# Ordering a kernel's first pass by a deadline plan, and moving part of a weight decode from VectorE to ScalarE

## The chip, the cores and the metric

The kernel runs on one core of a Trainium2 chip. TensorE (PE) multiplies, VectorE (DVE), ScalarE (ACT) and GpSimd (POOL) do elementwise work, and SyncE (SP) issues all DMA transfers. The metric is the time of one execution on the device in microseconds, as the median of several runs.

## The reference, cut to what matters

The core computes attention and then two MoE-like blocks, all in float32:

```
attn = softmax(scale * q k^T + alibi bias, causal window of 128) @ v     # 4 x 8 heads x 576 x 64
x  = attn reshaped to (2304 tokens, 512)
h  = x @ w_in;   g = h * cos(h);                     x2  = g @ w_out      # first MoE, d_ff 2048
h  = x2 @ w_in2; g = h if h >= 1, 0 if h <= -1, else (h+1)^2/4;  out = g @ w_out2
```

## The kernel before

**Precision.** Each matrix is split in a high and a low part (both float32r), and each product takes three matmuls: high times high, high times low, low times high. The weights come in as 8-byte floats (float64 bits) and are made into float32 by bit operations; this is called the decode here. A *half* is one tile of 128 by 512 of w_in or w_out; each MoE has 32 (index `j`; `f = j // 2` from 0 to 15, even `j` is w_in, odd `j` is w_out). Two forms of the decode exist. The form with three DVE operations scales the high words on ACT (L354, L868) and then runs shift-and-mask (L374, L870), or-in the sign (L385, L873) and or-in the low bits (L389, L876) on DVE. The form with two DVE operations adds a second ACT operation that makes the last bits from a 16-bit quarter (L358), a 16-bit mask on DVE (L372), and one combining DVE operation (L382). In the first MoE halves 0 to 3 use three and halves 4 to 31 two; all 32 halves of the second MoE use three. After the decode ACT writes the high part (a cast) and DVE the low part (`sub_lo`, L282).

**Attention** (to about 123 us) is ordered by hand; `make()` advances a generator (`halves()`) by one step at some places in it, so that nearly four halves are made there. At its end `put_x(p4, "A")` copies the last block on ACT and SP stores it.

**First pass**: the first 768 tokens (chunk 0 of the first MoE) without Strassen, for each `f`: `mm_a(0, f)` (512 tokens, 12 matmuls, into bank h0), `mm_b(0, f-1)`, `mm_a(1, f)` (256 tokens), `mm_b(1, f-1)`. Between `mm_a` and `mm_b` stands `chain`: k on ACT (L603), t on DVE (L605), sine on ACT (L607), the product on DVE (L609, the last reader of the bank), high part on ACT (L616), low part on DVE. There is one bank for `mm_a(0, f)`, so the next `mm_a(0, f+1)` waits for L609. Decode steps are put in by hand between the steps of a chain (`slot()`, `needed()`); `prep` (inputs of chunk (0,1): loads, subtractions on POOL at L756, high parts on ACT at L749, 14 low parts, here all on POOL) and `sum_steps` (sums of weight pairs 0 to 2, on POOL and ACT) are collected in `todo` and emitted whole at the end of a step `f`.

**The five other chunks** ((0,1), (0,2), (1,0), (1,1), (1,2): MoE, chunk) use one level of Strassen: seven products (L946) and the second matmul (L1007). Here `Plan` orders the work: PE's order is the program's, each other operation gets a due time from the PE operation that needs it, and a simulation with a price list (`COST`) starts on each engine the most urgent operation whose inputs are ready in the simulation. The order in which the operations start there becomes each engine's queue. Engines are free from 6.0 in its time, SP from 0. A 512 KB load occupies 1.65 of its bus and lands 4.5 later. Three `ld` buffers hold raw halves. `second_weights()` decodes the second MoE's weights from 45.0 + 33.0 per pair on.

Each engine executes its queue in order. An operation that waits for an input holds all that stand behind it.

Of the kernel before, what the change touches and what calls it, by code (L numbers as in the profile page):

```python
# [19 lines left out]
TWO_PI = 6.283185  # L20
# [11 lines left out]
ROUNDED = 4  # L32


def ops(m, j):

    return 2 if m == 0 and j >= ROUNDED else 3


N_W1 = sum(ops(0, j) + 1 for j in range(2 * NF))  # L40


def needed(j):

    return min(N_W1, sum(ops(0, i) + 1 for i in range(j)) + ops(0, j) + 2)


AHEAD = 3
EARLY = 3
# [3 lines left out]
D_TAIL = 5  # L53
# [48 lines left out]
class Plan:  # L102
# [4 lines left out]
    def op(self, eng, cost, fn, reads=(), writes=(), after=0.0, gate=(), step=0):  # L107
# [6 lines left out]
        for r in writes:  # L114
            if r.writer is not None:
                o.deps.add(r.writer)
            o.deps.update(r.readers)
            if isinstance(r, Buf) and not r.users:
                o.new.append(r)
            r.writer, r.readers = o, []  # L120
# [123 lines left out]
def attention_moe_moe_kernel(  # L244
# [48 lines left out]
    def stage_raw(m, j):  # L293

        if j < 2 * NF and (m, j) not in raw64:
# [40 lines left out]
    def halves():  # L336

        before = None  # L340

        def new_u(j):
            f = j // 2
            if j % 2:
                return two.tile([128, 512], F32, tag="wu", name=nm("wu"), bufs=U_BUFS)
            if f % 2 == 0:
                win_u[f // 2] = big("W", NF, "up", F32, (128, 4, 256)) if f < 12 else pair_tile()
            return half_u(win_u[f // 2], f)

        def first(j):  # L350
            stage_raw(0, j)
            low, high = words(raw64[0, j])
            u = new_u(j)
            ACT.activation(u, high.bitcast(F32), AF.Copy, scale=2.0**-112)  # L354
            if ops(0, j) == 2:


                ACT.activation(low.bitcast(I32), quarters(raw64[0, j])[:, :, 1], AF.Copy,  # L358
                               bias=0.5**14 - 0.5, scale=0.5**13)
            return u  # L360

        u = first(0)
        yield
        for j in range(2 * NF):
            stage_raw(0, j + 1)
            t = raw64.pop((0, j))
            low, high = words(t)
            ui = u32(u)
            if ops(0, j) == 2:

                q = quarters(t)
                DVE.tensor_single_scalar(out=q[:, :, 1], in_=q[:, :, 3], scalar=0x8000, op=ALU.bitwise_and)  # L372
            else:
                DVE.tensor_scalar(out=ui, in0=ui, scalar1=3, scalar2=0x7FFFFFFF,  # L374
                                  op0=ALU.logical_shift_left, op1=ALU.bitwise_and)
            yield
            if before:
                before()
                yield
            if ops(0, j) == 2:  # L380
                u_next = first(j + 1) if j + 1 < 2 * NF else None
                DVE.scalar_tensor_tensor(out=ui, in0=ui, scalar=3, in1=low,  # L382
                                         op0=ALU.logical_shift_left, op1=ALU.bitwise_or)
            else:
                DVE.scalar_tensor_tensor(out=ui, in0=high, scalar=0x80000000, in1=ui,  # L385
                                         op0=ALU.bitwise_and, op1=ALU.bitwise_or)
                yield
                u_next = first(j + 1) if j + 1 < 2 * NF else None
                DVE.scalar_tensor_tensor(out=ui, in0=low, scalar=29, in1=ui,  # L389
                                         op0=ALU.logical_shift_right, op1=ALU.bitwise_or)  # L390
            f, h = j // 2, j % 2
# [6 lines left out]
            def before(w=w, u=u, f=f, h=h):  # L398
                sub_lo(DVE, w[:, 1, :], u, w[:, 0, :])
                if not h:  # L400
                    p = f // 2
                    if f % 2:
                        if p >= EARLY:
                            stores.append(lambda: SP.dma_start(ud[p], win_u[p]))
                        stores.append(lambda: move(fd[0][p][3], w[:, :, 256:512]))
                    else:
                        stores.append(lambda: move(fd[0][p][0], w))

            yield
            u = u_next  # L410
        if before:
            before()
            yield

    making = halves()
    made = [0]
    started = [False]

    def start():

        if not started[0]:
            started[0] = True
            next(making)

    def make():

        start()
        if next(making, making) is not making:
            made[0] += 1


# [149 lines left out]
    c0 = {}  # L581

    def mm_a(i, f):
        tag = "h3" if f == 1 and i == 0 else f"h{i}"
        w = FIRST[i][1]
        h = ps.tile([128, 512], F32, tag=tag, name=nm("h"))[:, 0:w]
        n = 0
        for d in range(KD):
            xh, xl = x0[i, d]
            s = slice(d * 128, d * 128 + 128)  # L590
            for k, x in ((0, xh), (0, xl), (1, xh)):
                PE.matmul(h, lhsT=win[f][:, k, s], rhs=x, start=(n == 0), stop=(n == 11))  # L592
                n += 1
        c0["h", i, f] = h

    def chain(i, f):


        w, h = FIRST[i][1], c0.pop(("h", i, f))
        t = small("t")[:, 0:w]  # L600
        k = small("k", I32)[:, 0:w]

        ACT.activation(k, h, AF.Copy, bias=0.25, scale=INV_2PI)  # L603
        yield
        DVE.scalar_tensor_tensor(out=t, in0=h, scalar=INV_2PI, in1=k,  # L605
                                 op0=ALU.mult, op1=ALU.subtract)
        ACT.activation(t, t, AF.Sin, bias=half_pi, scale=TWO_PI)  # L607
        yield
        DVE.tensor_tensor(out=t, in0=h, in1=t, op=ALU.mult)  # L609
        if i:  # L610
            g = small("g", F32R)
            gh, gl = g[:, 0:w], g[:, w:2 * w]
        else:
            gh, gl = (small(s, F32R)[:, 0:w] for s in ("gh", "gl"))
        c0["g", i, f] = gh, gl
        ACT.copy(gh, t)  # L616
        yield
        sub_lo(DVE, gl, t, gh)

    def mm_b(i, f):  # L620
        if f == 0:
            w = FIRST[i][1]
            if i:
                b = [ps.tile([128, 512], F32, tag=f"h{2 + d}", name=nm("y")) for d in range(2)]
                c0["y", i] = [b[d // 2][:, d % 2 * w:d % 2 * w + w] for d in range(KD)]
            else:
                c0["y", i] = [ps.tile([128, 512], F32, tag=f"y{d}", name=nm("y"))[:, 0:w]
                              for d in range(KD)]
        gh, gl = c0["g", i, f]

        for d in range(KD):
            s = slice(d * 128, d * 128 + 128)
            for k, (a, x) in enumerate(((0, gh), (0, gl), (1, gh))):
                PE.matmul(c0["y", i][d], lhsT=wout[f][:, a, s], rhs=x,
                          start=(f == 0 and k == 0 and not (i and d % 2)),
                          stop=(f == NF - 1 and k == 2 and (i == 0 or d % 2 == 1)))

# [8 lines left out]
    def attention():  # L646
# [8 lines left out]
        for k in range(-AHEAD, np_ - AHEAD - 1):  # L655
# [35 lines left out]
            if k + 1 == D_STEPS[0]:  # L691
                start()
# [37 lines left out]
        for _ in range(D_TAIL - 2):  # L730
            make()
        put_x(p4, "A")

# [48 lines left out]
    def first_pass():  # L782

        todo = {}

        def later(eng, cost, fn, reads=(), writes=(), gate=(), step=0):
            new = [r for r in writes if isinstance(r, Buf) and not r.users]
            for r in new:
                r.users.append(None)

            def run():
                for r in new:
                    r.t = r.make()
                fn()

            todo.setdefault(step, []).append(run)

        bt = prep(later, 0, 1, "P", (), 5)
        for b in bt.values():
            for t in b:  # L800
                t.users.clear()
        for p in range(EARLY):
            s = Buf("W", None)
# [363 lines left out]
```

## Time and profile before

| | |
|---|---|
| median of 3 runs | 924.61 us (922.9 to 925.96) |
| profiled execution: its own time | 919.17 us |
| profiled execution: span | 917.4 us, granted clock 0.994 |
| PE busy | 882.2 us (96%) |
| DVE busy | 676.9 us (74%) |
| ACT busy | 534.9 us (58%) |
| POOL busy | 272.4 us (30%) |
| DMA | 190.29 MB, mean 207 GB/s |

The 2 us between the span and the execution's own time lie around the span. PE counts as busy also while it runs slower than it could, so the share of 96% says little; the stages have to be read apart. A name such as "DVE gl L282" is an engine, the tile written and the line.

### The profile page before, as it was taken

What the parts mean: (1) busy time and instruction counts of PE and PEld (TensorE: products, weight loads), DVE (VectorE), ACT (ScalarE), POOL (GpSimd) and SP (SyncE); (2) the same over time, 40 slices, a digit from 0 to 9 for tenths busy, and PEclk for the clock granted to TensorE, in tenths of its full rate; (3) what the DMA queues carried; (4) which work ended last, traced back from release to release, by engine and by line L of the source; (5) the groups of instructions that cost most, each with busy time, mean ns of one, the idle gap of its engine ahead of it and who ended that gap; (6) DMA issues with size and microseconds to landing.
All of it is one profiled execution on the core that took longest, in us unless ns stands there. A gap on an engine that the chain in (4) does not pass through costs nothing.

```text
span 917.4 us, 15799 instructions
## 1 busy us (share of the span) xinstructions
PE 882.2 (96%) x5472; PEld 829.1 (90%) x5472; DVE 676.9 (74%) x1429; ACT 534.9 (58%) x1225; POOL 272.4 (30%) x276
## 2 busy tenths in 40 slices
PE   7998999988899999899999999999999999999998
PEld 5776778877789999889999989999999999999998
DVE  7997888878867779988898998776555558355551
ACT  8886878767656666557666565555344445344440
POOL 5766730364334532671210760201200004000000
PEclk9999999999999999999999999999999999999999
DMA  9547545757569978759879769865155452444200
GB/s 321 166 146 232 186 159 176 259 204 248 171 212 322 333 284 298 240 204 347 298 249 336 243 218 341 291 203 176 52 195 161 165 160 82 138 161 161 93 35 34
DMA packets 81262, 190.29 MB, mean 207 GB/s; under 512 B 8224, under 2 KB 40992, under 8 KB 81184
## 3 DMA queue, kind: packets, MB, share of 16 engines
q1 hardware_dynamic: 81184, 189.30, 60.8%
q8 instruction: 43, 0.70, 0.3%
q14 instruction: 35, 0.29, 0.1%
HBM read 140.51 MB, written 48.76 MB: 206 GB/s over the span
## 4 chain that ended last, share of the span: by engine, by line
PE 49%; DVE 6%; issue 2%; ACT 1%; POOL 0%; DVEq 0%; ACTq 0%
PE y L1007 26%; PE h L946 24%; DVE gl L282 2%; DVE wu L873 1%; DVE wu L870 1%; DVE wo L282 1%; DVE up L870 0%; DVE b L282 0%; ACT gh L964 0%; DVE up L876 0%; POOL T L756 0%; ACT c L954 0%; DVE t L987 0%; DVE t L975 0%; DVE t L981 0%
## 5 line engine op out<-in xcount | busy, mean ns | idle before, releaser
L1007 PE MATMUL y<-gh,wo 128*128 128x384 f32 x1280 | 338.6, 335 | 0.0
L946 PE MATMUL h<-b,wi 128*128 128x384 f32 x1680 | 308.2, 336 | 6.2 <-DVE b L282 2.7
L946 PEld LDWEIGHTS h<-b,wi 128*128 128x128 f32 x1680 | 292.6, 188 | 9.8 <-ACT c L954 4.4
L1007 PEld LDWEIGHTS y<-gh,wo 128*128 128x128 f32 x1280 | 232.7, 188 | 0.1
L1007 PE MATMUL y<-gl,wo 128*128 128x384 f32 x640 | 214.8, 336 | 4.1 <-DVE gl L282 4.1
L1007 PEld LDWEIGHTS y<-gl,wo 128*128 128x128 f32 x640 | 120.4, 188 | 6.3 <-DVE gl L282 6.3
L954 ACT COPY c<-h 128x384 f32<-128x384 f32 x120 | 57.3, 477 | 92.2 <-PE h L946 88.3
L958 DVE TENSOR_TENSOR c<-h,c 128x384 f32<-128x384 f32 x120 | 66.4, 554 | 47.2 <-PE h L946 26.8
L324 POOL TENSOR_TENSOR up<-up 128x256 f32<-128x256 f32 x64 | 60.2, 943 | 129.8 <-DVE so L282 113.9
L984 ACT ACTIVATE t<-t,half 128x384 f32<-128x384 f32 x96 | 58.9, 617 | 56.5 <-DVE t L981 56.1
L282 DVE TENSOR_TENSOR gl<-t,gh 128x384 fp32r<-128x384 f32 (+1 forms) x96 | 61.2, 638 | 33.7 <-ACT gh L964 28.3
L592 PE MATMUL h<-x,wi 128*128 128x512 f32 (+1 forms) x384 | 75.1, 347 | 9.7 <-DVE t L609 9.7
L507 ACT ACTIVATE sc<-sc,st 128x256 f32<-128x256 f32 (+1 forms) x144 | 70.2, 489 | 21.1 <-DVE st L500 19.4
L513 POOL TENSOR_TENSOR sc<-sc,st 128x512 f32<-128x512 f32 (+1 forms) x72 | 70.0, 994 | 36.8 <-DVE st L644 24.4
L592 PEld LDWEIGHTS h<-x,wi 128*128 128x128 f32 x384 | 62.0, 195 | 19.3 <-DVE t L609 10.5
L756 POOL TENSOR_TENSOR xs<-xs,xs 128x384 f32<-128x384 f32 x20 | 25.4, 1270 | 172.0 <-DVE b L282 121.5
L282 POOL TENSOR_TENSOR so<-up,so 128x512 fp32r<-128x512 f32 x32 | 47.0, 1478 | 90.1 <-ACT so L328 90.1
L282 DVE TENSOR_TENSOR gl<-g,gh 128x384 fp32r<-128x384 f32 x80 | 55.0, 727 | 6.7 <-PE y L1007 3.1
L994 DVE TENSOR_TENSOR g<-c,t 128x384 f32<-128x384 f32 x80 | 48.0, 600 | 15.7 <-ACT t L984 10.1
L500 DVE CUSTOM_DVE_ANT_0 sc<-pa,dist 128x256 f32<-128x256 f32 (+1 forms) x144 | 52.5, 403 | 8.1 <-PE pa L485 7.8
L978 ACT ACTIVATE t<-t,half_pi 128x384 f32<-128x384 f32 x64 | 39.4, 616 | 27.1 <-DVE t L975 26.5
L964 ACT CAST gh<-t 128x384 fp32r<-128x384 f32 x80 | 41.1, 514 | 23.5 <-DVE t L987 22.6
(94 smaller groups left out, 1226.9 us busy)
## 6 DMA issues: line engine op xcount, KB each, us to landing
wi<-fd SPq DMA_DIRECT2D x120, 512.0 KB, 4.5
wst<-in_w SPq DMA_DIRECT2D x64, 512.0 KB, 4.7
fd<-so SPq DMA_DIRECT2D x40, 512.0 KB, 4.3
qk<-in_qkv SPq DMA_DIRECT2D x36, 320.0 KB, 3.6
wi<-fd SPq DMA_DIRECT2D x40, 256.0 KB, 3.1
xs<-xd SPq DMA_DIRECT2D x40, 192.0 KB, 4.0
v<-in_qkv SPq DMA_DIRECT2D x36, 192.0 KB, 3.8
out_t<-ys SPq DMA_DIRECT2D x24, 192.0 KB, 1.9
```

Of the source, the lines that this page charges most:

```text
L282: eng.tensor_tensor(out=out, in0=full, in1=f32(hi), op=ALU.subtract)
L324: op("P", "tt256", lambda i=i, x=x, y=y, alu=alu: POOL.tensor_tensor(out=s.t[:, i, :], in0=s.t[:, x, :], in1=s.t[:, y, :], op=alu), writes ...
L500: DVE.tensor_tensor_reduce(out=sc[:, h, 0:w], in0=b[h], in1=dist8[2 * hp + h][:, 256 - w:256], scale=-0.125, scalar=3.0e38, op0=ALU.add, o ...
L507: ACT.activation(sc[:, h, 0:w], sc[:, h, 0:w], AF.Exp, bias=st[:, c:c + 1], scale=-1.0, accum_out=st[:, 4 + c:5 + c])
L513: POOL.tensor_tensor(out=sc[:, :, 0:w], in0=sc[:, :, 0:w], in1=st[:, 8 + 2 * j:10 + 2 * j].unsqueeze(2).to_broadcast([128, 2, w]), op=ALU. ...
L592: PE.matmul(h, lhsT=win[f][:, k, s], rhs=x, start=(n == 0), stop=(n == 11))
L946: PE.matmul(cell.t, lhsT=unit.t[:, a, s], rhs=bs[kt].t[:, x, :], start=(start and i == 0), stop=(stop and i == 5), skip_group_check=True)
L954: op("A", "copy384", lambda: ACT.copy(s.t, cell.t), reads=[bank[tag]], writes=[s])
L958: op("D", "tt384", lambda: DVE.tensor_tensor(out=s.t, in0=cell.t, in1=s.t, op=ALU.add), reads=[bank[tag]], writes=[s])
L984: op("A", "f384", lambda: ACT.activation(t.t, t.t, AF.Square, bias=half, scale=0.5), writes=[t])
L994: DVE.tensor_tensor(out=g.t, in0=h.t, in1=t.t, op=alu)
L1007: PE.matmul(cell.t, lhsT=w[:, a, s], rhs=x.t, start=(first and i == 0 and k == 0), stop=(last and i == 1 and k == 2), skip_group_check=True)
```

## The change

The hand order of the first pass goes (`first_pass`, `slot`, `needed`, `later`). `rest` becomes `moes`: the first pass's matmuls, chains, decodes, `prep` and `sum_steps` are handed to the same `Plan` as the rest, ahead of the other chunks. PE's order stays as it was. In attention four halves are made to their end, their stores issued, and nothing of half 4. `prep` of chunk (0,1) splits its 14 low parts between DVE and POOL. The decode of the second MoE takes the form with two DVE operations, and starts at 178.0 + 33.0 per pair, in a plan whose time now begins at the end of attention.

```diff
+MADE = 4
+W2_FROM, W2_STEP = 178.0, 33.0
 COST: "A": + k512 (0.49, 0.66), f512 (0.57, 0.78), k256 (0.29, 0.43), f256 (0.41, 0.56)
       "D": + ts16 (0.72, 0.82)
...
 def halves():
-        for j in range(2 * NF):
-            stage_raw(0, j + 1)
+        for j in range(MADE):
+            stage_raw(0, j)
+            if j + 1 < MADE:
+                stage_raw(0, j + 1)
...
+            ACT.activation(u, high.bitcast(F32), AF.Copy, scale=2.0**-112)
             yield
+            DVE.tensor_scalar(out=ui, ..., op0=ALU.logical_shift_left, op1=ALU.bitwise_and)
+            yield
+            DVE.scalar_tensor_tensor(out=ui, in0=high, ...)
+            yield
+            DVE.scalar_tensor_tensor(out=ui, in0=low, ...)
...
+            ACT.copy(w[:, 0, :], u)
+            if before:
+                yield
+                low_part(*before)
+            before = f, h
...
 # end of attention()
         put_x(p3, "A")
         make()
-        for _ in range(D_TAIL - 2):
-            make()
+        for _ in making:
+            pass
         put_x(p4, "A")
+        while stores:
+            stores.pop(0)()
...
+    def moes():
-                    {"s": [13.0] * 7, "W": w_held, "B": [...],
-                     "Q": [6.0], "so": [8.0] * 2, "up": [9.0] * 2, "wu": [6.0] * 2})
+                    {"s": [8.0] * 4, "ld": [9.0], "wu": [8.0], **kept})
+        def decode(raw, u, ap):            # for both MoEs
+            op("A", "u512", lambda: ACT.activation(ap(), words(raw.t)[1].bitcast(F32), ...), reads=[raw], writes=[u])
+            op("A", "u512", lambda: ACT.activation(words(raw.t)[0].bitcast(I32), quarters(raw.t)[:, :, 1], ...), writes=[raw])
+            op("D", "ts16", lambda: DVE.tensor_single_scalar(out=quarters(raw.t)[:, :, 1],
+                in_=quarters(raw.t)[:, :, 3], scalar=0x8000, op=ALU.bitwise_and), writes=[raw])
+            op("D", "tt512", lambda: DVE.scalar_tensor_tensor(out=u32(ap()), in0=u32(ap()), scalar=3,
+                in1=words(raw.t)[0], ...), reads=[raw], writes=[u])
...
-                start = 45.0 + 33.0 * p
+                start = W2_FROM + W2_STEP * p
...
+        def first_weights(j):
+            raw = Buf("ld", ...)
+            op("S", "512", lambda: SP.dma_start(raw.t, w1[f, h]), writes=[raw])
+            ...
+            decode(raw, u, ap)
+            op("A", "hi512", ..., reads=[u], writes=[w])
+            op("D", "tt512", lambda: sub_lo(DVE, ...), reads=[u], writes=[w])
...
+        sum_steps(op, 0, 0, pair0, ...)
+        for f in range(NF):
+            if 2 * f >= MADE:
+                first_weights(2 * f)
+                first_weights(2 * f + 1)
+            mm_a(0, f)
+            chain(0, f)
+            if f:
+                mm_b(0, f - 1)
+            last = mm_a(1, f)
+            chain(1, f)
+            for g in (f - 2, f - 1) if f == 2 else (f - 1,) if f > 2 else ():
+                mm_b(1, g)
+            if f == 4:
+                bt = prep(op, 0, 1, "DP", [last])
         for p in range(EARLY, NP):
             s = Buf("up", pair_tile)
-            load_sum(op, p, s, ())
+            load_sum(op, p, s, [ud_res[p]])
...
         attention()
-        rest(first_pass())
+        moes()
```

## Rows read from the trace of the kernel before

**Rows 1.** Busy time by stage (us busy, x instructions, clock, DMA share, GB/s).
```profile
123.06:268.56 145.50, 134.66 (x747) 116.74 (x746) 120.13 (x183) 104.05 (x203) 49.65 (x40) 0.98 0.62 210
...
374.00:412.00 38.00, 33.07 (x183) 31.07 (x182) 35.31 (x45) 19.59 (x42) 28.07 (x23) 1.00 0.59 198
...
503.00:550.00 47.00, 44.18 (x240) 42.59 (x239) 43.95 (x56) 27.13 (x57) 32.34 (x27) 0.96 0.70 235
550.00:917.00 367.00, 363.98 (x2100) 363.66 (x2098) 212.31 (x419) 155.64 (x314) 24.96 (x22) 1.00 0.46 153
```

**Rows 2.** Timeline of PE, first pass (start us, us).
```profile
123.06 7.24 PE L592 MATMUL h<-x,wi 128*128 128x512 f32 x36
130.80 0.50 PE L634 MATMUL y<-gh,wo 128*128 128x512 f32 x1 [0.51 <-ACT gh L616]
...
146.38 2.91 PE L592 MATMUL h<-x,wi 128*128 128x512 f32 x12
...
154.72 2.91 PE L592 MATMUL h<-x,wi 128*128 128x512 f32 x12
...
192.11 4.37 PE L592 MATMUL h<-x,wi 128*128 128x512 f32 x12 [3.87 <-DVE t L609]
...
241.80 4.61 PE L592 MATMUL h<-x,wi 128*128 128x512 f32 x12 [2.68 <-DVE t L609]
...
268.56 1.21 PE L946 MATMUL h<-b,wi 128*128 128x384 f32 x6
```

**Rows 3.** Waits in 125 to 275 us (total, times, longest us).
```profile
PE h L592 <- DVE t L609: 9.7, 4, 3.9
```

**Rows 4.** Timeline of ACT in front of the longest stall.
```profile
186.89 0.51 ACT L749 CAST b<-xs 128x384 fp32r<-128x384 f32 x1 [2.98 <-POOL xs L756]
...
188.35 0.59 ACT L603 ACTIVATE k<-h 128x512 int32<-128x512 f32 x1
```

**Rows 5.** Timeline of ACT where attention ends.
```profile
122.62 0.68 ACT L354 ACTIVATE wu<-wst 128x512 f32<-128x512 f32 x1
123.20 0.61 ACT L396 CAST wi<-up 128x512 fp32r<-128x512 f32 x1
123.72 0.36 ACT L570 COPY x<-pa 128x256 f32<-128x256 f32 x1
126.21 0.60 ACT L603 ACTIVATE k<-h 128x512 int32<-128x512 f32 x1 [2.13 <-PE h L592]
126.95 0.68 ACT L354 ACTIVATE up<-wst 128x512 f32<-128x512 f32 x1
```

**Rows 6.** Timeline of SP's DMA queue, the same stretch.
```profile
123.12 0.42 SPq L297 DMA_DIRECT2D wst<-in_w  x1
124.11 0.32 SPq L574 DMA_DIRECT2D xd<-x  x1
```

**Rows 7.** DMA issues from 110 to 140 us (median us to landing).
```profile
wst<-in_w SPq DMA_DIRECT2D x5, 512.0 KB, 3.9
```

**Rows 8.** Lines of the decode: duration ns min/median/max, first and last start.
```profile
L372 DVE TENSOR_SCALAR wst<-wst x28: 729/761/1468, 128.2 to 253.9; 128x512 uint16<-128x512 uint16 x28
...
L382 DVE SCALAR_TENSOR_TENSOR wu<-wu,wst x14: 682/1506/1789, 135.2 to 255.7; 128x512 uint32<-128x512 uint32 x14
...
L870 DVE TENSOR_SCALAR up<-up x16: 415/424/1227, 324.9 to 567.5; 128x512 uint32<-128x512 uint32 x16
...
L876 DVE SCALAR_TENSOR_TENSOR up<-wst,up x16: 677/684/1501, 327.3 to 573.5; 128x512 uint32<-128x512 uint32 x16
...
L358 ACT ACTIVATE wst<-wst x28: 639/660/696, 127.5 to 253.3; 128x512 int32<-128x512 uint16 x28
```

**Rows 9.** Timeline of DVE at 190 us.
```profile
190.08 1.47 DVE L372 TENSOR_SCALAR wst<-wst 128x512 uint16<-128x512 uint16 x1 [0.42 <-ACT wst L358]
```

**Rows 10.** Timeline of POOL at 188 us.
```profile
188.45 2.51 POOL L282 TENSOR_TENSOR so<-up,so 128x512 fp32r<-128x512 f32 x2
```

**Rows 11.** Timeline of PE, end of chunk (0,1).
```profile
383.75 0.44 PE L1007 MATMUL y<-gl,wo 128*128 128x384 f32 x1 [1.62 <-DVE gl L282]
```

More of the change, by code (lines that the diff above doesn't have):

```diff
@@ L117, in op @@
             o.deps.update(r.readers)
-            if isinstance(r, Buf) and not r.users:
+            if isinstance(r, Buf) and not r.users and r.make:
                 o.new.append(r)
@@ L293, in stage_raw @@
     def stage_raw(m, j):
-        if j < 2 * NF and (m, j) not in raw64:
+        if (m, j) not in raw64:
             t = two.tile([128, 512], mybir.dt.int64, tag="ld", name=nm("wst"), bufs=LD_BUFS)
@@ L336, in halves @@
     def halves():
-        before = None
[L342 to L350, printed above, removed]
-            stage_raw(0, j)
[L352 to L360, printed above, removed]
@@ L380, in halves @@
[L380 to L390, printed above, removed]
@@ L391, in halves @@
-            f, h = j // 2, j % 2
+            if h:
+                wout_u[f] = u = two.tile([128, 512], F32, tag="wu", name=nm("wu"), bufs=U_BUFS)
+            else:
+                if f == 0:
+                    win_u[0] = big("W", NF, "up", F32, (128, 4, 256))
+                u = half_u(win_u[0], f)
+            ui = u32(u)
+            ACT.activation(u, high.bitcast(F32), AF.Copy, scale=2.0**-112)
+            yield
+            DVE.tensor_scalar(out=ui, in0=ui, scalar1=3, scalar2=0x7FFFFFFF,
+                              op0=ALU.logical_shift_left, op1=ALU.bitwise_and)
@@ L392, in halves @@
+            yield
+            DVE.scalar_tensor_tensor(out=ui, in0=high, scalar=0x80000000, in1=ui,
+                                     op0=ALU.bitwise_and, op1=ALU.bitwise_or)
+            yield
+            DVE.scalar_tensor_tensor(out=ui, in0=low, scalar=29, in1=ui,
+                                     op0=ALU.logical_shift_right, op1=ALU.bitwise_or)
             if h:
@@ L396, in halves @@
             ACT.copy(w[:, 0, :], u)
[L398 to L413, printed above, removed]
-    making = halves()
[L416 to L423, printed above, removed]
+            if before:
+                yield
+                low_part(*before)
+            before = f, h
+        yield
+        low_part(*before)
+    wout_u = {}
+    making = halves()
     def make():
-        start()
-        if next(making, making) is not making:
-            made[0] += 1
+        next(making, None)
     def kind(blk):
@@ L579, in attention_moe_moe_kernel @@
     half_pi2 = one.tile([128, 1], F32, name="half_pi2")
[L581 to L636, printed above, removed]
     def prepare(p):
@@ L780, in load_sum @@
         op("S", "512", lambda: SP.dma_start(s.t, ud[p]), reads=reads, writes=[s])
[L782 to L803, printed above, removed]
-            s.users.append(None)
-            early = lambda *a, step=0, p=p, **k: later(*a, step=step + 2 * p + 2, **k)
-            early("P", "", lambda s=s, p=p: setattr(s, "t", win_u[p]))
-            sum_steps(early, 0, p, s, lambda: Buf("so", part_tile), lambda i: Res())
-        def slot():
-            if made[0] < N_W1:
-                make()
-        for f in range(NF):
-            while made[0] < needed(2 * f):
-                make()
-            mm_a(0, f)
-            for _ in chain(0, f):
-                slot()
-            if f:
-                mm_b(0, f - 1)
-            mm_a(1, f)
-            for n, _ in enumerate(chain(1, f)):
-                if n:
-                    slot()
-            slot()
-            while made[0] < needed(2 * f + 1):
-                make()
-            for g in (f - 2, f - 1) if f == 2 else (f - 1,) if f > 2 else ():
-                mm_b(1, g)
-            for fn in todo.pop(f, ()):
-                fn()
-        for f in sorted(todo):
-            for fn in todo[f]:
-                fn()
-        while stores:
-            stores.pop(0)()
-        return bt
-    def rest(bt):
-        w_held = []
+    def moes():
         bank = {f"{k}{i}": Res() for k in "hy" for i in range(4)}
@@ L845, in rest, with ready @@
         wo = [[None] * NF for _ in range(2)]
-        for f in range(NF):
-            wo[0][f] = b = Buf("W", None)
-            b.t = wout[f]
-            w_held.append(b)
+        wi = [None] * NF
+        held = []
+        def ready(tag, t):
+            b = Buf(tag, None)
+            b.t = t
+            held.append(b)
+            return b
+        for f in range(2):
+            wo[0][f] = ready("W", wout[f])
+            wi[f] = ready("Q", win[f])
+        pair0 = ready("W", win_u[0])
         g_res = [Res() for _ in range(NF)]
@@ new lines, in moes, with mm_a, go @@
+        h_of, g_of, y_of = {}, {}, {}
+        def mm_a(i, f):
+            tag = "h3" if f == 1 and i == 0 else f"h{i}"
+            w = FIRST[i][1]
+            cell = h_of[i, f] = Cell()
+            def go():
+                cell.t = h = ps.tile([128, 512], F32, tag=tag, name=nm("h"))[:, 0:w]
+                n = 0
+                for d in range(KD):
+                    xh, xl = x0[i, d]
+                    s = slice(d * 128, d * 128 + 128)
+                    for k, x in ((0, xh), (0, xl), (1, xh)):
+                        PE.matmul(h, lhsT=wi[f].t[:, k, s], rhs=x, start=(n == 0), stop=(n == 11))
+                        n += 1
+            cell.res = bank[tag]
+            return op("PE", f"b{w}", go, reads=[wi[f]], writes=[cell.res])
@@ new lines, in chain @@
+        def chain(i, f):
+            w, h = FIRST[i][1], h_of.pop((i, f))
+            t, k = Buf("s", lambda: small("t")[:, 0:w]), Buf("s", lambda: small("k", I32)[:, 0:w])
+            op("A", f"k{w}", lambda: ACT.activation(k.t, h.t, AF.Copy, bias=0.25, scale=INV_2PI),
+               reads=[h.res], writes=[k])
+            op("D", f"tt{w}", lambda: DVE.scalar_tensor_tensor(
+                out=t.t, in0=h.t, scalar=INV_2PI, in1=k.t, op0=ALU.mult, op1=ALU.subtract),
+               reads=[h.res, k], writes=[t])
+            op("A", f"f{w}", lambda: ACT.activation(t.t, t.t, AF.Sin, bias=half_pi, scale=TWO_PI), writes=[t])
+            op("D", f"tt{w}", lambda: DVE.tensor_tensor(out=t.t, in0=h.t, in1=t.t, op=ALU.mult),
+               reads=[h.res], writes=[t])
+            if i:
+                gs = [Buf("s", lambda: small("g", F32R))]
+                part = lambda n: gs[0].t[:, n * w:n * w + w]
+            else:
+                gs = [Buf("s", lambda: small("gh", F32R)), Buf("s", lambda: small("gl", F32R))]
+                part = lambda n: gs[n].t
+            g_of[i, f] = gs, part
+            op("A", f"hi{w}", lambda: ACT.copy(part(0), t.t), reads=[t], writes=gs[:1])
+            op("D", f"tt{w}", lambda: sub_lo(DVE, part(1), t.t, part(0)), reads=[t, gs[0]], writes=gs[-1:])
@@ new lines, in mm_b, with go @@
+        def mm_b(i, f):
+            w = FIRST[i][1]
+            tags = ["h2", "h3"] if i else [f"y{d}" for d in range(KD)]
+            gs, part = g_of.pop((i, f))
+            def go():
+                if f == 0:
+                    b = [ps.tile([128, 512], F32, tag=tag, name=nm("y")) for tag in tags]
+                    y_of[i] = [b[d // 2][:, d % 2 * w:d % 2 * w + w] if i else b[d][:, 0:w] for d in range(KD)]
+                for d in range(KD):
+                    s = slice(d * 128, d * 128 + 128)
+                    for k, (a, x) in enumerate(((0, 0), (0, 1), (1, 0))):
+                        PE.matmul(y_of[i][d], lhsT=wo[0][f].t[:, a, s], rhs=part(x),
+                                  start=(f == 0 and k == 0 and not (i and d % 2)),
+                                  stop=(f == NF - 1 and k == 2 and (i == 0 or d % 2 == 1)))
+            return op("PE", f"b{w}", go, reads=[wo[0][f], *gs], writes=[bank[t] for t in tags])
```

115 lines of the change are left out of this document (65 added, 50 removed), and 4 rows, old and new, of the table COST.

## Prediction

> **What bounds the kernel now.** I read the busy time by stage first. From 550 us on PE runs 2100 matmuls of 384 columns in 363.98 us, 0.1733 us each, with no stage below that pace but the last few microseconds [rows 1]: nothing that only reorders work can gain there. The losses lie ahead of it. In 374 to 412 us, where chunk (0,1) hands over to (0,2), 183 matmuls need 31.7 of 38 us: 6.3 lost. In 503 to 550 us, the hand-over from (0,2) to (1,0), 240 need 41.6 of 47: 5.4 lost. In both DVE is busy for 93% of the time (35.31 of 38, 43.95 of 47) [rows 1], and PE's waits there are for a low part on DVE [rows 11].
>
> The first pass runs from 123.06 to 268.56 us, 145.5 us [rows 1, 2]. PE's timeline gives its undisturbed step: `mm_a(0, f)` starts at 146.38 and the next at 154.72, 8.34 us apart. There are 16 groups `mm_a` and 15 groups `mm_b`, two of which make a step: 15.5 x 8.34 = 129.3 us. So 16.2 us are lost. Four waits of `mm_a` for the product L609 make 9.7 of them [rows 3]. After the two longer ones (3.87 and 2.68 us) the 12 matmuls take 4.37 and 4.61 us where others take 2.91 [rows 2], and the granted clock of the pass is 0.98 and not 1.00 [rows 1]: 3.2 more, 12.9 in all. The other 3.3 lie at the start and in small pieces.
>
> Why L609 is late, ACT's timeline shows: ACT stood 2.98 us in front of a cast of `prep` that waited for POOL's subtraction, and the k of the chain, which needs only PE, came behind it at 188.35 [rows 4]. The longest wait, 3.87 us, follows from that. It is a fault of the order, not of the amount of work: ACT is busy for 104.05 of 145.5 us and DVE for 120.13 [rows 1].
>
> **The change, part by part.** *The order of the first pass.* `Plan` starts an operation only when its inputs are ready in its simulation, so a cast that needs POOL isn't put ahead of a k that is ready. The four waits go: 12.9 us off. Bounds: 0 if all come back in another place, 12.9; I take the full amount, since ACT has 41 us to spare in the pass and the plan knows what each cast waits for.
>
> *The start of the first pass.* Here the plan is wrong about SP. It lets SP issue the loads of halves 4 and 5 at its time 0, six units before PE, and has them land before k of `chain(0, 0)` is ready; so ACT's queue gets u of half 4, its last bits, u of half 5, and only then k. On the chip SP's queue stands behind attention's last transfers. Before, the load of half 4 was issued at 123.12, ahead of the store of `put_x(p4)` at 124.11 [rows 6]; now it comes behind that store. And `put_x(p4)` itself, an ACT copy at 123.72 [rows 5], now comes behind all of half 3: u 0.68, from about 123.2, then shift, sign and low bits on DVE (0.42, 0.68, 0.68 by their medians [rows 8]), the cast 0.61, the copy 0.36 [rows 5], and about 0.5 of hand-overs: 127.1. Then three issues of about 0.4 each [rows 6] (the x store, a store of half 2's factor, the load of half 4) bring that load to about 128, and 3.9 us to landing [rows 7] to about 132; half 5 is there by 132.6, its u done by 133.3. k of `chain(0, 0)` then starts at 133.3 instead of 126.21 [rows 5]. From k to `mm_b(0, 0)` it took 4.59 us (130.80 [rows 2]), so that group starts at 137.9. PE has work until about 130.2 and now waits 7.7 us instead of 0.5: 7.2 more, and 1.5 for the clock after such a wait (4.37 against 2.91 [rows 2]). Cost: 8.7. Bounds: 0, if the loads are there in time, and 8.7. Behind k on ACT stand the sine and the high part of the same chain, and PE waits for them. The halves 4 and on lose nothing more, since PE waits longer than they do.
>
> *`prep`'s low parts.* Seven go from POOL to DVE. No row gives one alone; the DVE operations of 512 columns bound it by 0.42 and 1.50 us [rows 8]: 3 to 10.5 us for seven, I take 6.4, near 0.9 each. DVE idles for 25.4 us of the pass [rows 1], which hides them; without that cover they cost what the third rival says. Finishing half 3 inside attention moves three DVE operations of about 0.7 us forward by 2 to 3 us, behind which the chain waited anyway.
>
> *The second MoE's decode.* Per half L870, L873 and L876 go (0.42 + 0.69 + 0.68 = 1.79 us by their medians, L873 priced like L876) and L372 and L382 come (0.76 + 0.68, the least of L382): 0.35 us less DVE. When POOL runs beside them the longest are 1.23 + 1.50 + 1.50 = 4.23 against 1.47 + 1.51 (L382's median) = 2.98: 1.25 less [rows 8]. The stretches that start a pair (four halves) every 33 us hold 4.6 and 5.7 halves: 1.6 to 5.8 us in the first, 2.0 to 7.1 in the second. Both are bound by DVE, so I take the low end as the gain, 3.6 together; the bounds are 0 and 11.7, all that is lost there. ACT pays 0.66 us (L358) for each of 32 halves, 21 us, hidden under its idle time (19.59 busy of 38, 27.13 of 47 [rows 1]). If that cover is gone, a half comes late, and it is next needed only in chunk (1,0), or when a third raw buffer has to come free.
>
> One row speaks for how much of this is saved. L372 at 190.08 took 1.47 us while POOL ran a low part from 188.45 to 190.96 [rows 9, 10], twice its median of 0.76: as if it waited for POOL, although it reads one tile. The Trainium skill ("SBUF — State Buffer", Who interferes with whom) says that a DVE instruction with at most one SBUF input outside the two-port modes does not contend with GpSimd, and that one with two SBUF inputs does. By that rule L372 would cost 0.76 beside POOL too, and the saving there would be 1.96 us a half and not 1.25. The row goes against it, so the sum stays by rows.
>
> Where the second MoE's decode starts hardly moves: 172 after PE's start in the new plan, 39 after the start of chunk (0,1) in the old one, and the first pass is 129.3 to 145.5 long.
>
> Sum: -12.9 + 8.7 - 3.6 = -7.8 us. On the profiled execution 919.17 gives 911.4; that execution is 5.4 below the median, so on the median's scale 924.61 gives 916.8.
>
> **The rivals.**
>
> *No wait at the start.* If the load of half 4 lands before k is ready, the 8.7 us don't come: 924.61 - 12.9 - 3.6 = 908.1. For it: before, that load landed by 126.95, when its u began without waiting [rows 5]. Against it: the order of SP's queue.
>
> *Other waits take the place of the old ones.* The plan's queues are fixed by its prices; where an operation takes twice its price, as beside POOL [rows 8], what stands behind it is late. If the start costs 8.7, and one wait of the old kind with its slow clock (3.87 + 1.5) is left, the time is 924.61 - 7.8 + 5.4 = 922.2, and with the gain at the hand-overs gone too 925.8; I put the case at 924, no change that can be measured.
>
> *DVE becomes the bound of the first pass: slower.* DVE has 120.13 us of work there, and 6.4 are added: 126.5 [rows 1]. At today's share of 83% that takes 153 us, 7.7 more than now, less 3.6 later: 928.7. The plan also may pull sums of pairs 3 and up into the pass, and their POOL time stretches DVE's. It decides when DVE can't be kept busy for more than 126.5 / 149.1 = 85% of the pass. Against it: in the two hand-overs DVE was kept busy for 93%.
>
> **How the numbers follow.** Forecast (start costs, waits gone, 912 to 921): 0.42. No wait at the start (904 to 911): 0.20. Other waits (921 to 927): 0.17. DVE the bound (927 to 932): 0.15. Outside these, 0.06, mostly below 904 or a worse hand-over. About 0.3%, 2.8 us, is what a measurement of this kernel can tell from no change. Faster than 921.8: nearly all of the first two and a quarter of the third, 0.68; same 0.16; slower 0.16. The range 904 to 926 leaves out DVE the bound and little else; the forecast's own is 912 to 921.
>
> **What would show it.** In the changed kernel's trace: the load of half 4 issued after the store of `put_x(p4)`; ACT's k of `chain(0, 0)` behind two u's, near 133; `mm_b(0, 0)` near 138; no wait over 1 us of `mm_a` for L609's successor after that, and from there steps of 8.34; DVE's idle time in the pass small but there; at the two hand-overs PE's loss down from 6.3 and 5.4 to about 8 together. The prediction is wrong if `mm_b(0, 0)` starts before 133, if waits for DVE are spread over the pass, or if the second half of the kernel, from 550 us on, does not keep its pace.

## The result, and the profile after

The changed kernel takes 914.04 us (median; 912.6 to 916.26) and the kernel before, in the same rounds, 924.37 (922.9 to 925.96): a ratio of 0.989, 95% interval 0.9864 to 0.9916. The forecast was 916.8. The total came out, but by luck: two of its terms were each off by about 6 us, in opposite directions.

Busy time by stage of the kernel after, its stages cut like those of [rows 1]: the first pass, then 105.45 us, the first hand-over, 91 us, the second hand-over, and the rest (columns as there).

```profile
127.47:275.05 147.58, 133.66 (x746) 115.97 (x745) 130.09 (x190) 107.95 (x211) 68.25 (x59) 0.98 0.74 253
275.05:380.50 105.45, 104.88 (x606) 104.05 (x604) 78.61 (x138) 71.92 (x146) 17.83 (x18) 1.00 0.75 254
380.50:418.50 38.00, 37.40 (x211) 36.19 (x211) 35.11 (x44) 24.34 (x52) 26.87 (x21) 1.00 0.67 236
418.50:509.50 91.00, 91.00 (x527) 91.00 (x526) 74.33 (x129) 67.44 (x137) 17.10 (x16) 1.00 0.85 296
509.50:556.50 47.00, 44.62 (x244) 43.32 (x243) 42.45 (x55) 26.77 (x56) 27.44 (x24) 0.96 0.74 251
556.50:914.40 357.90, 354.52 (x2046) 354.20 (x2044) 204.87 (x402) 155.63 (x314) 27.50 (x22) 1.00 0.45 150
```

And two stretches of the kernel before that [rows 1] leave out:

```profile
268.56:374.00 105.44, 103.70 (x591) 101.31 (x590) 83.87 (x138) 67.40 (x139) 39.49 (x36) 1.00 0.86 307
412.00:503.00 91.00, 90.23 (x520) 89.78 (x519) 78.29 (x143) 62.10 (x126) 18.04 (x17) 1.00 0.87 306
```

The first pass takes 147.58 us against 145.5 [rows 1, 2]: it became 2.1 longer, where 4.2 less were forecast. From its end to the end of the span it is 639.4 us against 917.4 - 268.56 = 648.8: 9.5 less, where 3.6 were forecast. The matmul counts say where: in stretches as long as before, PE gets through 15, 28, 7 and 4 matmuls more. At 0.1733 us each [rows 1] that is 2.6, 4.9, 1.2 and 0.7 us, 9.4 in all. The last stage keeps its pace.

PE's timeline at the start of the first pass (as [rows 2]):

```profile
127.47 7.20 PE L786 MATMUL h<-x,wi 128*128 128x512 f32 x36
142.09 0.79 PE L825 MATMUL y<-gh,wo 128*128 128x512 f32 x1 [7.43 <-ACT gh L810]
...
147.02 3.21 PE L786 MATMUL h<-x,wi 128*128 128x256 f32 x19
```

SP's DMA queue at the end of attention (as [rows 6]):

```profile
118.09 13.31 SPq L518 DMA_DIRECT2D xd<-x  x6
131.49 0.62 SPq L278 DMA_DIRECT2D fd<-wi  x1
132.16 7.10 SPq L747 DMA_DIRECT2D wst<-in_w  x4
```

ACT's timeline there (as [rows 5]):

```profile
130.69 0.36 ACT L514 COPY x<-pa 128x256 f32<-128x256 f32 x1
136.17 0.66 ACT L700 ACTIVATE up<-wst 128x512 f32<-128x512 f32 x1 [5.12 <-DMA wst<-in_w]
136.74 0.63 ACT L702 ACTIVATE wst<-wst 128x512 int32<-128x512 uint16 x1
137.28 0.58 ACT L795 ACTIVATE k<-h 128x512 int32<-128x512 f32 x1
```

Read these from bottom to top. PE's 7.43 us wait is for the chain of k, and k is ready work: its matmuls ended near 130. It stands behind two operations on half 4, these behind a load, and the load at 132.16 behind the stores of a factor and of attention's last block, whose copy ACT makes only at 130.69. No engine is short of time there (from 127.47 to 142.09 DVE is busy for 6.87 of 14.62 us and ACT for 6.51); by this reading the order of two queues makes the wait, which e1, e5, e9 and e10 test. The granted clock of 142.09 to 147.02 is 0.58, near the lower level of 1.2 GHz, after PE stood still.

The waits of PE in the pass (columns as [rows 3]) show that the wait for t, L609 then and L801 now, fell from 9.7 to 4.5 us, in five pieces of at most 1.5:

```profile
PE y L825 <- ACT gh L810: 7.4, 1, 7.4
PE h L786 <- DVE t L801: 4.5, 5, 1.5
PE y L825 <- DVE g L271: 1.9, 2, 1.0
```

### The profile page after: what moved, and what is told of

Read it like the earlier page. It is cut to its first block, busy times and chain, and to the rows that moved or that the text cites. A ratio compares the mean times of both kernels' runs of the same rounds, so it can differ in the third digit from the quotient of the medians.

```text
span 914.4 us, 15792 instructions
## 1 busy us (share of the span) xinstructions
PE 882.4 (96%) x5472; PEld 832.2 (91%) x5472; DVE 668.9 (73%) x1404; ACT 552.9 (60%) x1257; POOL 264.2 (29%) x269
## 5 line engine op out<-in xcount | busy, mean ns | idle before, releaser
L313 POOL TENSOR_TENSOR up<-up 128x256 f32<-128x256 f32 x64 | 62.2, 972 | 212.2 <-DVE so L271 170.2
L786 PE MATMUL h<-x,wi 128*128 128x512 f32 (+1 forms) x384 | 72.3, 339 | 4.5 <-DVE t L801 4.5
L786 PEld LDWEIGHTS h<-x,wi 128*128 128x128 f32 x384 | 59.9, 190 | 13.8 <-DVE t L801 5.8
L271 DVE TENSOR_TENSOR gl<-g,gh 128x384 fp32r<-128x384 f32 x80 | 59.3, 778 | 7.2 <-PE y L937 3.1
L705 DVE TENSOR_SCALAR wst<-wst 128x512 uint16<-128x512 uint16 x60 | 52.3, 871 | 10.9 <-ACT wst L702 10.4
```

What stands on the lines that cost most here:

```text
L271: eng.tensor_tensor(out=out, in0=full, in1=f32(hi), op=ALU.subtract)
L313: op("P", "tt256", lambda i=i, x=x, y=y, alu=alu: POOL.tensor_tensor(out=s.t[:, i, :], in0=s.t[:, x, :], in1=s.t[:, y, :], op=alu), writes ...
L705: op("D", "ts16", lambda: DVE.tensor_single_scalar(out=quarters(raw.t)[:, :, 1], in_=quarters(raw.t)[:, :, 3], scalar=0x8000, op=ALU.bitwi ...
L786: PE.matmul(h, lhsT=wi[f].t[:, k, s], rhs=x, start=(n == 0), stop=(n == 11))
```

## The experiments

For each run, from its profile: the length of the first pass, the time from there to the end of the span ("later part"), and the timed ratio to the kernel before. c0_after is the changed kernel run once more, as a yardstick. A ratio is taken to the kernel before in the same rounds; its median there was 924.37 us for after, 921.31 for e1 to e4, 922.20 for c0_after, e5, e7 and e8, and 920.50 for e9 to e11. So compare ratios, not medians.

| run | pass | later part | median us | ratio (95%) |
|---|---|---|---|---|
| before (span 917.4) | 145.5 | 648.8 | 924.37 | 1 |
| after (span 914.4) | 147.6 | 639.4 | 914.04 | 0.989 (0.9864 to 0.9916) |
| c0_after | 148.3 | 639.4 | 913.18 | 0.9903 (0.9889 to 0.9918) |
| e1_loads_early | 145.3 | 638.6 | 910.91 | 0.988 (0.9861 to 0.9898) |
| e2_decode3 | 148.8 | 645.2 | 919.23 | 0.9965 (0.995 to 0.9979) |
| e3_before_decode2 | 145.6 | 641.7 | 914.38 | 0.9912 (0.9894 to 0.9929) |
| e4_sums_late | 142.2 | 639.8 | 909.95 | 0.986 (0.984 to 0.9879) |
| e5_sp_time | 155.4 | 638.6 | 919.99 | 0.9981 (0.9965 to 0.9997) |
| e7_k_first | 141.5 | 645.5 | 910.27 | 0.9868 (0.9851 to 0.9885) |
| e8_prep_pool | 150.6 | 639.3 | 918.73 | 0.9956 (0.9938 to 0.9973) |
| e9_sum0_held | 135.9 | 640.0 | 902.48 | 0.98 (0.9774 to 0.9825) |
| e10_plan_times | 138.8 | 638.0 | 902.04 | 0.9804 (0.9778 to 0.983) |
| e11_dve_back | 144.9 | 651.8 | 923.82 | 1.0031 (1.0013 to 1.0049) |

My theory after the result: the decode's DVE time makes the gain, the order of the start and POOL's work inside the pass eat what the planned order brings. The rival: the planned order makes the gain and the decode little.

**The two parts, each alone: e2, e3.** e2 is the changed kernel with the old decode of the second MoE:

```diff
-                decode(raw, u, ap)
+                decode3(raw, u, ap)    # u512 on ACT; ts512, tt512, tt512 on DVE
```

> The changed kernel, with the second MoE decoded by three DVE operations again and nothing else undone. Theory A (the hand-overs gained by fewer DVE operations): PE's loss in the hand-over from chunk (0,1) to (0,2), 1.4 us now against 6.3 before the change, returns by 3 us or more, and the kernel takes about 918 to 921. Theory B (they gained by the new order and the pair sums that moved into the first pass): the loss stays under 3 us and the time is 913 to 916.

e3 is the kernel before with the new decode in `second_weights`, and the price of `ts16` in the plan (shortened):

```diff
-  ts512, tt512, tt512 on DVE
+  op("A", "u512", ...)   # last bits on ACT
+  op("D", "ts16", ...)
+  op("D", "tt512", ...)
```

> The kernel before the change, with the second MoE decoded by two DVE operations and one more ACT operation: that part of the change alone. Theory A (decode): the hand-over from chunk (0,1) to (0,2) loses 2 us or less of PE time instead of 6.3, and the kernel takes about 917 to 920. Theory B (order): 922 to 925.

The decode alone gives 0.88%, about 8 us, and everything but the decode (e2, called the order here) 0.35%; together 1.2%, about what the whole change gives. In e2 the pass is 3.3 us longer than in the kernel before, the later part 3.6 shorter. Why the order alone shortens the later part was not taken apart. The times speak for theory A, its sign at the first hand-over less so: by the matmul count at 0.1733 us PE's loss there returns from 1.4 to 4.0 us in e2 (196 matmuls), a little less than expected, and in e3 it is 5.4 (188 matmuls) and not under 2. The two hand-overs of e3 (stages as above):

```profile
374.21:412.21 38.00, 34.70 (x188) 33.78 (x188) 33.85 (x41) 22.31 (x47) 25.68 (x23) 0.96 0.61 207
503.21:550.21 47.00, 45.99 (x262) 44.89 (x261) 45.87 (x59) 30.38 (x62) 30.92 (x25) 1.00 0.74 255
```

Here the second one gains (262 matmuls for 240), in the kernel after it is the first (211 for 183). The split between the two depends on the order and stays open.

**Is it DVE's time? e11.** e3, with one DVE operation given back per half that leaves the bits as they are:

```diff
+  op("D", "ts512", lambda: DVE.tensor_scalar(out=u32(ap()), in0=u32(ap()),
+      scalar1=0, scalar2=0xFFFFFFFF, op0=ALU.logical_shift_left, op1=ALU.bitwise_and))
   op("D", "ts16", ...)
   op("D", "tt512", ...)
```

> The kernel before with the new decode of the second MoE, which alone gave a ratio of 0.991, and one DVE operation more per half (a shift by 0 and a mask of ones, 0.42 us), so that DVE's work per half is that of the kernel before. If DVE's time is what the decode saved, the gain goes: ratio 0.996 to 1.002. If it came from something else in the new form (the order that the plan makes of it, or shorter use of the raw buffers), the ratio stays at 0.990 to 0.994.

The gain is gone: 1.0031, just above the expected range, and a later part of 651.8 against 641.7 of e3. ACT's operation was still in, so the gain goes with DVE's operations and not with ACT's. The added operation also holds the raw buffer longer and changes the plan's order; the run doesn't separate these. How far DVE's time fell, the groups of DVE's instructions show (busy us, mean ns). Before, for 32 halves in 290 to 620 us:

```profile
L873 DVE SCALAR_TENSOR_TENSOR wu<-wst,wu 128x512 uint32<-128x512 uint32 x16 | 13.5, 851 | 0.2
L876 DVE SCALAR_TENSOR_TENSOR wu<-wst,wu 128x512 uint32<-128x512 uint32 x16 | 13.3, 837 | 0.1
L876 DVE SCALAR_TENSOR_TENSOR up<-wst,up 128x512 uint32<-128x512 uint32 x16 | 12.6, 785 | 0.0
...
L873 DVE SCALAR_TENSOR_TENSOR up<-wst,up 128x512 uint32<-128x512 uint32 x16 | 11.9, 741 | 0.3
L870 DVE TENSOR_SCALAR wu<-wu 128x512 uint32<-128x512 uint32 x16 | 9.7, 606 | 0.5 <-ACT wu L868 0.5
...
L870 DVE TENSOR_SCALAR up<-up 128x512 uint32<-128x512 uint32 x16 | 8.8, 548 | 1.3 <-ACT up L868 1.3
```

After, in 300 to 620 us:

```profile
L705 DVE TENSOR_SCALAR wst<-wst 128x512 uint16<-128x512 uint16 x32 | 26.4, 824 | 4.0 <-ACT wst L702 3.8
...
L708 DVE SCALAR_TENSOR_TENSOR wu<-wu,wst 128x512 uint32<-128x512 uint32 x16 | 17.8, 1139 | 0.0
...
L708 DVE SCALAR_TENSOR_TENSOR up<-up,wst 128x512 uint32<-128x512 uint32 x16 | 11.5, 720 | 0.1
```

69.8 against 55.7 us: 14.1 us, 0.44 a half. PE gained 9.4 us from these 14.1 and from the order. In e11 the decode takes DVE longer than in the kernel before:

```profile
L876 DVE TENSOR_SCALAR wst<-wst 128x512 uint16<-128x512 uint16 x32 | 27.1, 855 | 0.6 <-ACT wst L870 0.2
...
L879 DVE SCALAR_TENSOR_TENSOR wu<-wu,wst 128x512 uint32<-128x512 uint32 x16 | 15.4, 962 | 0.1
...
L879 DVE SCALAR_TENSOR_TENSOR up<-up,wst 128x512 uint32<-128x512 uint32 x16 | 14.5, 906 | 0.1
...
L873 DVE TENSOR_SCALAR wu<-wu 128x512 uint32<-128x512 uint32 x16 | 10.1, 638 | 0.5 <-ACT wu L868 0.5
...
L873 DVE TENSOR_SCALAR up<-up 128x512 uint32<-128x512 uint32 x16 | 9.2, 576 | 1.1 <-ACT up L868 0.9
```

That is 76.3 us, 6.5 more than before, and its later part is 3.0 us longer. In e3 the same groups take 54.8 us, 15.0 less, and the later part is 7.1 us shorter; in e2 they take 66.2, 10.5 more than in the kernel after, and the later part is 5.9 us longer. In all three pairs a microsecond of DVE in the decode is worth about half a microsecond of the later part (0.46, 0.47, 0.56), which is the best support here for DVE's time as the cause.

**The start: e1, e5.** e1 issues the loads of halves 4 and 5 in attention's tail, as the kernel before did with half 4:

```diff
+        for j in range(MADE, MADE + 2):
+            stage_raw(0, j)
...
+            raw = early_raw.get(j)
+            if raw is None: ...    # else no load here
```

> The changed kernel, with the raw halves 4 and 5 loaded ahead of the last copy and store of attention, and told to the plan as already there. Theory (SP's queue order makes the start wait): mm_b(0,0) starts within 4 us of the end of the third mm_a instead of 7.4 us after it, the PE wait of 7.4 us and the slow matmuls after it (about 2 us) go, and the kernel runs in about 905 to 907 us. Rival (the wait is ACT's and DVE's backlog from attention, or the decode of later halves is then late instead): a wait of more than 4 us stays or comes back within the first steps, and the time stays above 911.

ACT's timeline in e1:

```profile
128.83 0.67 ACT L703 ACTIVATE up<-wst 128x512 f32<-128x512 f32 x1 [0.39 <-DMA wst<-in_w]
130.14 0.66 ACT L703 ACTIVATE wu<-wst 128x512 f32<-128x512 f32 x1 [0.64 <-DMA wst<-in_w]
130.70 1.21 ACT L705 ACTIVATE wst<-wst 128x512 int32<-128x512 uint16 x2
131.80 0.59 ACT L800 ACTIVATE k<-h 128x512 int32<-128x512 f32 x1
```

The loads now hardly stop ACT, and k starts 6.95 us after PE's first `mm_a` (124.85 in e1) instead of 9.81; it still stands behind four operations on halves 4 and 5. PE's wait falls to 4.38 us and not to nothing, and the waits for t rise to 7.2 us in six pieces. The ratio can't be told from c0_after's, and the expected 905 to 907 us were missed. The late load makes 3 of the 7.4 us of wait; the rest is order, as e9 and e10 show, where k goes first.

e5 tells the plan that SP is free only at 11.0:

```diff
-        free["S"] = 0.0
+        free["S"] = 11.0
```

> The changed kernel, with SP free from 11.0 instead of 0 in the plan's time and nothing else changed: the loads go out when they did, but ACT gets k of chain(0,0) ahead of the decode of half 4. Theory (the plan's wrong belief about SP sets ACT's order, and this order makes the wait): the wait of 7.4 us in front of mm_b(0,0) falls under 1.5 us, a wait of 1 to 4 us may come in front of mm_a(0,2), and the first pass is 4 to 8 us shorter than the changed kernel's. Rival (data or backlog, not order): mm_b(0,0) still waits more than 4 us. A second rival: the start is mended, and waits for DVE later in the pass take back most of it, as with the early loads; first pass within 3 us of the changed kernel's.

The start is nearly mended (waits 2.89, 0.48 and 0.98 us, with under 1.5 expected for the first; what is left of it is the cast met in e7 below), and the expected shorter pass did not come: the kernel is 0.8% slower than c0_after. One wait of PE late in the pass takes more than the start gave:

```profile
261.24 3.36 PE L786 MATMUL h<-x,wi 128*128 128x512 f32 x7 [8.96 <-ACT wi L759]
```

The cast waited for is that of half 28, the first of the last weight pair (the expectation of e10 calls it half 30). Its u stands late in ACT's queue, behind casts (L317) of a pair's sums:

```profile
253.72 0.61 ACT L317 CAST so<-up 128x512 fp32r<-128x512 f32 x1
...
256.19 0.65 ACT L700 ACTIVATE up<-wst 128x512 f32<-128x512 f32 x1
```

In the code the last two w_in pairs of the first MoE are made in a buffer "up", of which there are two, and the pair sums are loaded into the same two; SP issued such loads (L667) at 238.91 and 243.84. So sums that the plan has pulled forward hold the buffer that the last weights need. This is argued from code and rows; in e10, which differs from e5 only in when sums run, the wait is gone.

**POOL's work in the pass: e4, e8.** e4 keeps the sums of pairs 3 on out of the pass:

```diff
-        op("S", "512", lambda: SP.dma_start(s.t, ud[p]), reads=reads, writes=[s])
+        op("S", "512", lambda: SP.dma_start(s.t, ud[p]), reads=reads, writes=[s], after=133.0)
```

> The changed kernel, with the pair sums 3 to 7 of the first MoE held back until the first pass is over, as before the change. Theory (their POOL work stretches DVE operations in the first pass and makes its remaining waits): the waits of mm_a and mm_b for DVE in the first pass, 6.4 us now, fall to 3 or less, and the pass is 3 to 6 us shorter; the stretch of chunk (0,1) after it loses up to 3 us more. Time 909 to 914. Rival (prep alone makes these waits): first pass as long as now, time 914 to 918.

The pass of e4, and PE's waits for t in it:

```profile
122.83:265.06 142.23, 132.62 (x746) 115.86 (x745) 120.68 (x190) 104.09 (x203) 44.31 (x39) 0.98 0.65 223
```

```profile
PE h L786 <- DVE t L801: 1.5, 2, 1.3
```

The same 190 DVE instructions take 120.68 us here and 130.09 in the kernel after; POOL has 20 instructions less. The waits for t fall from 4.5 to 1.5 us, and the pass from 148.3 in c0_after to 142.2. The later part doesn't pay for it: 639.8 against 639.4, though POOL is busy for 36.19 us in the 105.44 after the pass, where it was 17.83. So it is not the sums drawn into the pass that shorten the later part of the changed kernel. Two groups of DVE in the pass, first in the kernel after, then in e4:

```profile
L705 DVE TENSOR_SCALAR wst<-wst 128x512 uint16<-128x512 uint16 x28 | 25.9, 925 | 6.9 <-ACT wst L702 6.7
...
L708 DVE SCALAR_TENSOR_TENSOR wu<-wu,wst 128x512 uint32<-128x512 uint32 x14 | 12.2, 868 | 0.1
```

```profile
L705 DVE TENSOR_SCALAR wst<-wst 128x512 uint16<-128x512 uint16 x28 | 23.8, 852 | 6.0 <-ACT wst L702 5.8
...
L708 DVE SCALAR_TENSOR_TENSOR wu<-wu,wst 128x512 uint32<-128x512 uint32 x14 | 9.7, 696 | 0.0
```

e8 gives `prep`'s seven low parts back to POOL:

```diff
-                bt = prep(op, 0, 1, "DP", [last])
+                bt = prep(op, 0, 1, "P", [last])
```

> The changed kernel, with all 14 low parts of prep on POOL again. If these seven DVE operations crowd DVE, the first pass's waits for DVE (6.4 us) fall by 2 us or more; if POOL's longer work stretches DVE instead, they stay or grow, and the time is that of the changed kernel or up to 4 us more.

0.5% slower than c0_after, the pass 2.3 us longer, with POOL busy for 75.07 us. DVE has seven operations less and is busy for 129.74 us against 130.39 in c0_after: what it hands over it loses again while POOL runs longer. In e4 the DMA traffic falls along with POOL's work (DMA share 0.74 to 0.65); in e8 it doesn't rise (0.73 in c0_after, 0.70 in e8), so traffic doesn't explain DVE's slower operations there.

**k first, and the plan's times: e7, e9, e10.** e7 is e1 and e4 together, and the first ACT operation on halves 4 and 5 isn't before 10.0:

```diff
+            decode(raw, u, ap, 10.0 if j in early_raw else 0.0)    # after= of the first u512
```

> Three changes to the changed kernel together: halves 4 and 5 loaded ahead of the last copy of attention, their decode not before 10.0 in the plan's time (so k goes first), and the pair sums 3 to 7 held back until the first pass is over. If the start wait and the POOL work of the sums are separate losses, the first pass falls to 131 to 135 us and the ratio to the kernel before to 0.975 to 0.980. If other waits for DVE take the place of the start wait, the pass stays above 139 and the ratio at 0.985 or more.

k now starts 3.5 us after PE, but the next ACT operation in the queue is a cast of the pair sums, and it waits for POOL:

```profile
126.83 0.60 ACT L800 ACTIVATE k<-h 128x512 int32<-128x512 f32 x1
130.45 0.62 ACT L317 CAST so<-up 128x512 fp32r<-128x512 f32 x1 [3.02 <-POOL up L313]
```

That is the fault of [rows 4] in another place: the sine of the chain stands behind the cast, and PE waits 3.14 us. The pass gets to 141.5, not the expected 131 to 135, while the later part loses 6.1 us, a loss that e9 does not have and that was not explained.

e9 is e7 with that sum held back, and e10 is the changed kernel with nothing but three times set in the plan: SP's of e5, e4's 133.0, and this one:

```diff
+   after=16.0 if m == 0 and p == 0 else 0.0     # POOL's sums of pair 0
```

> The run with k first, halves 4 and 5 loaded early and the pair sums 3 to 7 late, and in addition the sums of pair 0 not before 16.0 in the plan's time. In the run without that, ACT stood 3.0 us behind k in front of the cast of pair 0's sum, which waited for POOL, and mm_b(0,0) waited 3.1 us. Theory (each of these waits is an operation that the plan believes ready and that isn't): mm_b(0,0) waits under 1 us, its matmuls run at 0.23 us each at once, and the first pass falls from 141.5 to 135 to 138 us. Rival (the chain itself, or DVE's backlog of half 3, makes that wait): it stays over 2 us and the pass over 140.

> The changed kernel with three times put right in the plan and not one transfer moved in attention: SP free from 11.0, pair 0's sums not before 16.0, the pair sums 3 to 7 not before 133.0. With SP's time alone, a wait of 9 us for half 30 had come near the end of the pass, with the sums of later pairs in front of it; theory: with these sums late it is gone, the start costs 2 to 4 us (half 4 lands late for mm_a(0,2)) instead of 9, and the pass takes 134 to 139 us; ratio to the kernel before 0.975 to 0.983. Rival (a late decode as such makes the 9 us): a wait of over 5 us for a cast of weights stays in the pass.

PE's timeline in e9, then in e10:

```profile
130.41 0.50 PE L831 MATMUL y<-gh,wo 128*128 128x512 f32 x1
```

```profile
130.02 0.50 PE L826 MATMUL y<-gh,wo 128*128 128x512 f32 x1
...
137.17 0.73 PE L787 MATMUL h<-x,wi 128*128 128x512 f32 x2 [2.13 <-ACT wi L760]
```

In e9 `mm_b(0, 0)` starts without a wait, and the pass takes 135.9 us, 6.6 above the 129.3 of its undisturbed steps. In e10 the wait moves to the first matmul that needs half 4, 2.13 us. Both end near 902 us, 0.98 of the kernel before and 1% below the changed kernel.

## Why the prediction was right, and where it wasn't

*The four waits, -12.9.* Right in its cause and mis-sized: -6.8. The 16.2 us of loss before, less the wait of 0.51 at the start, are 15.7; of the 18.3 after (147.6 - 129.3), 7.43 of wait and 2.0 of slow clock belong to the start (the 12 matmuls from 142.09 to 147.02 take 4.93 us against the 2.91 of [rows 2]), and 8.9 remain. The stall of [rows 4] did not come back in the middle of the pass. What came in its place is what two of the rivals named: the plan took sums of pairs 3 on into the pass (POOL 49.65 to 68.25 us), the same work took DVE longer, 130.09 instead of the rival's 126.5, and PE waits for it in seven small pieces, 6.4 us. e4 shows that price. I had named this mechanism and left it out of the sum. By the prediction's own signs this part was wrong: waits for DVE are spread over the pass, and the longest wait for t is 1.5 us and not under 1.

*The start, +8.7.* Right in place and size: 7.43 - 0.51 + 2.0 = 8.9. The load was issued 4.7 us after PE's start (forecast 4.9), k started after 9.8 (10.2), `mm_b(0, 0)` after 14.6 (14.8). One detail was wrong: k stood behind one u and its last bits, not behind two u's. The rival "no wait at the start" did not hold. What its 8.7 us would have been worth was not measured alone: e9 and e10, which take away this wait and the sums, win 9.5 to 12.4 us of the pass against c0_after, and e4, which takes away the sums only, wins 6.1; that leaves 3.4 to 6.3 for the start, less than its own loss.

*`prep`'s low parts, nothing.* The value was wrong, since it asked only whether DVE had time. DVE pays nothing (e8), but POOL's seven operations less are worth about 2.3 us in the pass, 0.5% in all. These 2.3 us are among the 6.8 above, so the order by itself gave less than 6.8.

*The second MoE's decode, -3.6.* The cause was right, the size not: in the later part -7.1 us alone (e3), with the order -9.5. By e2, 3.6 of these 9.5 come from the order, which the sum put at nothing outside the first pass, and 5.9 from the decode. The saving per half is 0.44 us, close to the 0.35 of the low end. The mistake was to count it only in the two hand-overs, for some ten halves; it is there for all 32, and the stretches that I took for full gained 3.8 us too (decode and order together).

*The total.* By profiles: attention +4.4 us, pass +2.1, later part -9.5, in all -3.0; and in c0_after 0.0, +2.8, -9.5, in all -6.7. The medians differ by 10.3 and 9.0 (924.37 and 922.20 less 914.04 and 913.18). The profiled execution of before was 5.4 us faster than its median, that of c0_after only 0.6, so a part of the timed gain is in no profile shown here. The forecast of -7.8 hit by luck, because -12.9 was 6.1 too much and -3.6 was 5.9 too little.

## What to carry to other kernels

A planner's order is as good as what it believes about when each queue becomes free: three wrong times (SP free at once, a sum's cast ahead of the first chain, sums drawn into a full stage) cost this kernel 1%, as much as the whole change brought (e10). Where an engine is bound in pieces all along, count a saving over all its instructions and not only in the stretches that look worst: here about half of it came through. And price work on POOL by what it does to DVE beside it. A total that comes out is no proof of its terms: take stretches apart.

## What the runs showed of the hardware

DVE's 16-bit mask, which reads one tile, again took twice its usual time beside POOL. DVE in the kernel after:

```profile
216.85 1.46 DVE L705 TENSOR_SCALAR wst<-wst 128x512 uint16<-128x512 uint16 x1
```

POOL in the same stretch:

```profile
216.67 1.01 POOL L643 TENSOR_TENSOR T<-xs,T 128x384 f32<-128x384 f32 x1 [0.50 <-DVE b L271]
217.64 1.11 POOL L313 TENSOR_TENSOR up<-up 128x256 f32<-128x256 f32 x1
```

Its median over 60 is 0.756 us, its longest 1.724. The 37 that no POOL instruction overlaps take 0.73 to 0.78 us, and each of the 13 above 0.9 us runs beside POOL. The prediction took such a row to go against a rule; it need not. The rule (the Trainium skill, "SBUF — State Buffer", Who interferes with whom) holds for instructions outside the two-port modes, and the same section names `tensor_scalar`, which the mask is, among those that can enter such a mode and then contend with GpSimd. In which mode the mask ran no run here shows, and what the two share wasn't measured by itself.

Attention varies by itself. Its code is the same in c0_after as in the kernel after, and it takes 123.02 and 127.47 us, the same 1105 matmuls at a granted clock of 1.00 and 0.97:

```profile
0.00:123.02 123.02, 112.58 (x1105) 84.06 (x1105) 102.92 (x450) 98.79 (x348) 79.35 (x112) 1.00 0.61 200
```

```profile
0.00:127.47 127.47, 116.35 (x1105) 87.45 (x1105) 103.41 (x450) 98.83 (x348) 79.21 (x112) 0.97 0.60 193
```

e11, with the attention of the kernel before (123.06 us there), has 126.57. So such a difference between two profiles says nothing of a change, and stages have to be compared from their own start.
